# An S5 scan gated by a GeGLU block, rebuilt around token-major gates, DMA transposes and a planned engine order

## The chip, the cores and the metric

The kernel runs on one core of a Trainium2 chip. The metric is the device time of one execution in microseconds (us). Engine names: PE is TensorE, DVE is VectorE, ACT is ScalarE, POOL is GpSimd, SP is SyncE; SP computes nothing here and issues DMAs.

## The reference

x has 2048 tokens of 512 channels, bf16; the hidden width of the feed-forward block is 1376.

```python
xn = _layernorm(x)                                  # per token, no affine
Lam_bar = exp(dt * Lam)                             # 512 complex states
Bu = xn @ B_bar.T                                   # B_bar = ((Lam_bar - 1) / Lam)[:, None] * B
h[t] = Lam_bar * h[t-1] + Bu[t]                     # along 2048 tokens
s = 2 * (h @ C.T).real + xn * Dskip
g = silu((gelu(xn @ w_gate) * (xn @ w_up)) @ w_down)
out = x + s * g
```

## The kernel before

The tokens are cut into four slabs of 512 (`s`), each slab into four tiles of 128 tokens (`m`), and everything is done slab by slab. The complex recurrence is done as a real one: the rotation by the angle of `Lam_bar` is taken out with cosine and sine tables (`cos_b`, `sin_b`, L519 to L524), so that DVE's scan instruction (L382) runs on real and imaginary parts apart with the decay `rho`; a second rotation turns the result back into `hst`.

Per slab, in the order of the code: `u_pair` (L336) multiplies the normalised, transposed input `xnT` with `BT`, 32 matmuls, and ACT copies the result into `U` (L341); `chain` queues DVE's work on it (two products and two sums, L352 and L356, four scans, L382, and the same rotation again) for the two halves `h` of the states; `ffn` does the gates channel-major: for each of 11 blocks of 128 hidden channels four matmuls for gate (L418) and four for up (L423) with the 512 tokens as the moving operand, a Gelu and a copy on ACT (L428, L430), and a product on DVE (L431) which writes `at`, already with channels on the partitions as `down` needs them; `y_mm` makes `y` of the slab before with 8 matmuls from `hst` (L457) and 4 narrow ones which add the skip term by a diagonal matrix `diagI` (L462); `down` (L438) does 11 matmuls per token tile, then Tanh on ACT (L443) and a fused product on DVE (L445), which together are twice the silu; `epi` multiplies, adds x and stores (L475, L476, L479).

The order of PE, ACT and SP is the order of the code. DVE's order comes from a small hand-written clock: `dve()` issues a step at the PE time it was given, and `later()` keeps the scan's steps waiting until they fit in between. PSUM is three pools: four banks `mm`, two `f`, two `y`.

At the start, B's two halves come over ACT's queue (L91) and are transposed on PE (`b_transposes`, L142) while x, the small vectors, then the weights come over SP's queue; slab 0's first PE work of substance is `u_pair(0, 0)`, after its four tiles have been normalised (L164) and transposed on PE (L173). C is transposed by DMA on SP (L511), and so is the normalised input of slabs 1 to 3 (L506). A DMA from SP or ACT takes one of eight completion counters in turn, in the order in which both engines' DMAs stand in the program, and the ninth waits for the first to land: in listings of the order such a wait is written `waits DMAHW0_49`.

## Time and profile before

| | |
|---|---|
| median of 3 runs | 205.35 us (205.35 to 206.63) |
| span of the profiled execution, first to last instruction | 203.5 us |
| outside the span (median less span) | 1.85 us |
| PE, DVE, ACT busy | 184.6, 166.4, 114.5 us |

The profile is of one execution and its times are from the span's start; 1.85 us of the median lie outside of it. A busy PE is not PE at its peak: the profile's matmul durations overlap, so that PE's work is better read from the distance between starts. The chain of waits follows the execution back from its last instruction and says at each step what was waited for.

### The profile page before, as it was taken

How to read it: one execution, taken by the hardware profiler on the slowest of the kernel's cores; microseconds unless marked ns; L12 is line 12 of the kernel's file. 1: busy time of each engine (PE TensorE's matmuls, PEld its weight loads, DVE VectorE, ACT ScalarE, POOL GpSimd, SP SyncE). 2: the span in 40 equal slices, each digit the busy share in tenths (PEclk: the TensorE clock that was granted, in tenths of full speed). 3: DMA queues.
4: the chain of work that ended last, by engine and by line, in shares of the span. 5: the costliest groups of instructions: out<-in, count | busy, mean ns of one | idle time of the engine just before them, and what ended most of it. 6: DMA issues, size and time to landing. Idle time of an engine off the chain costs nothing.

```text
span 203.5 us, 2555 instructions
## 1 busy us (share of the span) xinstructions
PE 184.6 (91%) x903; PEld 86.6 (43%) x903; DVE 166.4 (82%) x283; ACT 114.5 (56%) x207; POOL 14.2 (7%) x31
## 2 busy tenths in 40 slices
PE   5617999996999999999599999999799999999992
PEld 1603344442444444454244444454344444454441
DVE  1427799999999898999999988999419999994443
ACT  2695486892777897751147997751256644441210
POOL 2001603100000015000000014000000000000000
PEclk9975799999999999999999999999999999999999
DMA  6999963220000000222000000231000000000001
GB/s 192 300 368 357 182 140 122 48 57 0 0 3 0 0 0 25 45 63 52 26 0 5 0 0 27 52 76 30 26 0 0 0 3 26 26 26 26 29 26 53
DMA packets 20988, 12.26 MB, mean 60 GB/s; under 512 B 11408, under 2 KB 20976, under 8 KB 20976
## 3 DMA queue, kind: packets, MB, share of 16 engines
q1 hardware_dynamic: 19920, 11.05, 19.7%
q10 hardware_dynamic: 1056, 1.05, 1.6%
q8 instruction: 7, 0.11, 0.2%
q14 instruction: 5, 0.04, 0.1%
HBM read 7.38 MB, written 2.10 MB: 47 GB/s over the span
## 4 chain that ended last, share of the span: by engine, by line
PE 43%; DVE 36%; ACT 14%; DMA 2%; issue 2%; POOL 1%; ACTq 0%
PE f_ps L438 13%; PE u_ps L336 10%; DVE Ft L382 7%; PE y_ps L457 7%; PE up_ps L423 6%; PE g_ps L418 6%; ACT junk L489 5%; DVE at L431 4%; DVE pp L352 3%; DVE qq L352 3%; DVE yg L475 3%; ACT ub L430 3%; DMA Bn<-in_A_B_re_dram 2%; DVE hst L356 2%; DVE Wt L356 2%
## 5 line engine op out<-in xcount | busy, mean ns | idle before, releaser
L418 PE MATMUL g_ps<-xnT,wg 128*128 128x512 bf16 (+1 forms) x176 | 45.2, 379 | 0.2 <-ACT gt L428 0.2
L423 PE MATMUL up_ps<-xnT,wu 128*128 128x512 bf16 (+1 forms) x176 | 45.2, 379 | 0.0
L438 PE MATMUL f_ps<-wd,at 128*128 128x512 bf16 (+1 forms) x176 | 39.4, 379 | 5.5 <-DVE g L445 3.2
L428 ACT ACTIVATE gt<-g_ps 128x512 bf16<-128x512 f32 (+1 forms) x44 | 26.2, 595 | 16.2 <-PE g_ps L418 14.0
L336 PE MATMUL u_ps<-xnT,BT 128*128 128x512 bf16 x128 | 30.8, 403 | 0.5 <-DVE xnT L211 0.5
L443 ACT ACTIVATE th<-f_ps 128x512 f32<-128x512 f32 x16 | 9.6, 597 | 38.5 <-PE f_ps L438 38.5
L382 DVE TENSOR_TENSOR_SCAN Ft<-rho,it,Wt 128x512 bf16<-128x512 f32 x24 | 30.4, 1275 | 0.0
L457 PE MATMUL y_ps<-C,hst 128*128 128x512 bf16 x128 | 30.2, 379 | 0.0
L430 ACT ACTIVATE ub<-up_ps 128x512 bf16<-128x512 f32 (+1 forms) x44 | 26.3, 597 | 7.0 <-PE up_ps L423 7.0
L438 PEld LDWEIGHTS <-at 128*128 128x128 bf16 (+1 forms) x176 | 17.0, 98 | 26.4 <-issue 3.7
L423 PEld LDWEIGHTS <-wu 128*128 128x128 bf16 (+1 forms) x176 | 17.6, 100 | 20.4
L418 PEld LDWEIGHTS <-wg 128*128 128x128 bf16 (+1 forms) x176 | 17.2, 100 | 18.7 <-issue 0.5
L341 ACT ACTIVATE U<-u_ps 128x512 bf16<-128x512 f32 x32 | 18.9, 597 | 9.2 <-PE u_ps L336 9.1
L431 DVE TENSOR_TENSOR at<-gt,ub 128x512 bf16<-128x512 bf16 (+1 forms) x44 | 18.0, 412 | 3.4 <-ACT ub L430 3.4
L336 PEld LDWEIGHTS <-BT 128*128 128x128 bf16 x128 | 13.2, 103 | 17.5 <-issue 3.8
L445 DVE SCALAR_TENSOR_TENSOR g<-th,f_ps 128x512 f32<-128x512 f32 x16 | 10.8, 679 | 11.0 <-ACT th L443 11.0
L457 PEld LDWEIGHTS <-hst 128*128 128x128 bf16 x128 | 12.3, 98 | 14.4 <-DVE hst L356 0.5
L475 DVE TENSOR_TENSOR yg<-y_ps,g 128x512 bf16<-128x512 f32 x16 | 10.9, 679 | 2.3 <-PE y_ps L462 2.2
L352 DVE TENSOR_TENSOR pp<-U,cos_b 128x2048 bf16<-128x2048 bf16 x8 | 9.8, 1220 | 2.9 <-ACT U L341 2.8
L356 DVE TENSOR_TENSOR hst<-pp,qq 128x1024 bf16<-128x1024 bf16 x16 | 10.6, 686 | 0.2
L356 DVE TENSOR_TENSOR Wt<-pp,qq 128x1024 bf16<-128x1024 bf16 x16 | 10.6, 685 | 0.1
L504 ACT ACTIVATE xn<-x_tok,nb,rs 128x512 bf16<-128x512 bf16 x12 | 9.7, 809 | 1.6 <-POOL nb L537 1.6
(104 smaller groups left out, 151.6 us busy)
## 6 DMA issues: line engine op xcount, KB each, us to landing
out_dram<-ot SPq DMA_DIRECT2D x16, 128.0 KB, 1.7
x_tok<-in_A_x_dram SPq DMA_DIRECT2D x3, 512.0 KB, 4.9
wd<-in_B_w_down_dram SPq DMA_DIRECT2D x1, 1280.0 KB
Bn<-in_A_B_re_dram ACTq DMA_DIRECT2D x1, 512.0 KB, 4.9
x_tok<-in_A_x_dram SPq DMA_DIRECT2D x2, 256.0 KB, 4.5
Bn<-in_A_B_im_dram ACTq DMA_DIRECT2D x1, 512.0 KB, 6.6
wg<-in_B_w_gate_dram SPq DMA_DIRECT2D x1, 512.0 KB, 5.7
wu<-in_B_w_up_dram SPq DMA_DIRECT2D x1, 512.0 KB
```

The costliest lines, as they stand in the source:

```text
L336: nc.tensor.matmul(u_ps[:, :], lhsT=BT[:, ri, kt, pt * P : (pt + 1) * P], rhs=xnT[:, kt, cols], start=(kt == 0), stop=(kt == KT - 1),)
L341: ACT(out=U[:, ri, q, :], in_=u_ps[:, :], func=AF.Copy)
L352: TT(out=box[key][:], in0=src()[:], in1=tab[:, hs, :].unsqueeze(1).to_broadcast(W), op=ALU.mult)
L356: return lambda: TT(out=dst()[i], in0=box["pp"][:, i, :, :], in1=box["qq"][:, 1 - i, :, :], op=op)
L382: nc.vector.tensor_tensor_scan(out=box["F"][:, ri, q, :], data0=rho[:, pt : pt + 1].to_broadcast([P, TS]), data1=box["W"][:, ri, q, :], in ...
L418: nc.tensor.matmul(g_ps[:fs, :], lhsT=wg[:, kt, fsl], rhs=xnT[:, kt, cols], start=(kt == 0), stop=(kt == KT - 1))
L423: nc.tensor.matmul(u_ps[:fs, :], lhsT=wu[:, kt, fsl], rhs=xnT[:, kt, cols], start=(kt == 0), stop=(kt == KT - 1))
L428: ACT(out=gt[:fs], in_=g_ps[:fs, :], func=AF.Gelu_apprx_tanh)
L430: ACT(out=ub[:fs], in_=u_ps[:fs, :], func=AF.Copy)
L431: dve(now() + 0.9, 0.34, lambda: TT(out=at[:fs, j, :], in0=gt[:fs], in1=ub[:fs], op=ALU.mult))
L438: nc.tensor.matmul(f_ps[:, :], lhsT=at[:fs, k, m0 : m0 + P], rhs=wd[:fs, k, :], start=(k == 0), stop=(k == NFT - 1))
L457: nc.tensor.matmul(y_ps[:, :], lhsT=hst[:, j // NPT, j % NPT, m0 : m0 + P], rhs=C2[:, j // NPT, j % NPT, :], start=(j == 0), stop=False,)
```

## The change

Nearly every line is new. What changes in the work:

- **Gates token-major.** A tile of 128 tokens is now the stationary operand and the weights move: per tile 4 x 2 matmuls over 512 columns, twice, and 4 x 2 over the last 352 columns (1376 = 512 + 512 + 352). The product `at` then has tokens on the partitions, and `at_t` turns it into `atT` with a DMA transpose on SP's queue (11 blocks of 128 x 128 per tile; slab 0 in pieces of 8 and 3).
- **Wide steps.** PSUM is three slots of two banks and two banks for `y`. ACT empties two banks with one instruction of 1024 elements; `down` does two tiles per slot; a rotation is one DVE product of 4096 elements and one sum of 2048 (in slab 0 two sums of 1024), with a table of four parts `tab`.
- **Silu** is one ACT instruction (in place of Tanh and the DVE product), with a table set other than Gelu's.
- **Skip term.** DVE makes `sk = xn * Dskip` per tile, ACT copies it into y's PSUM bank, and the 8 matmuls accumulate onto it; `diagI` and its matmuls are gone. The first two tiles add it on DVE.
- **Start.** B is transposed by DMA on SP's queue. ACT's queue brings the first two thirds of w_gate and w_up; POOL's queue brings the vectors, `Drow`, slab 1 of x, the last third and w_down. Slab 0's gates come before its `u`: tile 0 is only centred, transposed, and scaled by ACT as it leaves PSUM. `rs` and `rho` come from powers on POOL.
- **Order.** Each step is recorded with its engine, an assumed cost and what it reads and writes. `Plan.run` list-schedules them forwards and backwards in 12 rounds and emits the best schedule by start time. PE's order is that of the code; ACT's, DVE's, POOL's and SP's are the plan's.

The core of the diff (the recorder's calls are kept where they order the work):

```diff
+    def run(self):
...
+        for _ in range(ROUNDS):
+            start, length = self._pass(deps, [p + r for p, r in zip(prio, rank)], True)
...
+        for i in sorted(range(n), key=lambda i: (start[i], i)):
+            self.steps[i][2]()
...
-        th = work.tile([P, D], FP32, name="th", tag="th")
-        ACT(out=th[:], in_=f_ps[:, :], func=AF.Tanh, scale=0.5)
...
-        for kt in range(KT):
-            nc.tensor.matmul(
-                y_ps[:, kt * P : (kt + 1) * P], lhsT=xnT[:, kt, mg : mg + P], rhs=diagI[:, kt, :],
-                start=False, stop=(kt == KT - 1),
-            )
...
+    load_w(ACT, nc.scalar, 0, 4.5, not_before=0.72, rank=200.0)
...
+    slots = [psum.tile([P, 2, D], FP32, name=f"slot{i}") for i in range(3)]
+    ybank = [psum.tile([P, D], FP32, name=f"ybank{i}") for i in range(2)]
...
+    dummies(9)
+    stats(0, 0)
+    xc = xn[0]
+    dve(512, lambda: V.tensor_scalar(out=xc[:], in0=x_tok[:, 0, :], scalar1=mv[:, 0, 0, 0:1], scalar2=None, op0=ALU.subtract),
+        [("x", 0, 0), ("mv", 0, 0)], [("xc",)], rate=2.3)
+    transposed(xc, 0, xcT[:], [("xc",)], [("xcT",)], 0, DVE)
...
+        for kind, (nm, wt, dst) in enumerate((("wg", wg, gt[q]), ("wu", wu, ub[q]))):
+            i, ps = slot()
+            for c in range(2):
+                pe(KT, 512, mm(ps, c, wt, c), [("xnT", s % 2, m), (nm, c)], [("slot", i, c)])
+            fn = AF.Gelu_apprx_tanh if kind == 0 else AF.Copy
+            acts(1024, lambda ps=ps, dst=dst, fn=fn: act(out=dst[:, 0:1024].rearrange("p (c w) -> p c w", c=2), in_=ps[:, :, :], func=fn),
...
+    def at_t(s, m, c0, c1):
+        j = (s * M + m) % NAT
+        k0, k1 = CK[c0][0], CK[c1][1]
+        dma(SP, 0.3 * (k1 - k0), 1.6, lambda: nc.sync.dma_start_transpose(
+            out=atT[:, k0:k1, m * P : (m + 1) * P], in_=at[j][:, k0 * P : k1 * P]),
...
+        acts(1024, lambda: act(out=g2[gi][:, :, :], in_=ps[:, :, :], func=AF.Silu),
...
+        if seed:
+            acts(512, lambda: act(out=bank[:], in_=sk[s % 2][:, m, :], func=AF.Copy), [("sk", s % 2, m)], [("y", i)])
...
+                         start=(j == 0 and not seed), stop=(j == 2 * NPT - 1), skip_group_check=True)
...
+        def rot(src, table, reads):
+            dve(4096, lambda: V.tensor_tensor(out=Qf, in0=src.unsqueeze(1).to_broadcast(WQ), in1=table, op=ALU.mult),
+                reads, ["Q"], rate=2.0)
...
+            dma(SP, 1.3, 2.2, lambda ri=ri, k=k, src=src: nc.sync.dma_start(out=BT[:, ri, k, :], in_=src[:, k * P : (k + 1) * P], transpose=True),
...
+    load_w(ACT, nc.scalar, 1, 9.0, rank=199.0)
...
+    for m in range(M):
+        gate_pair(0, m, 0, (lambda m=m: head_t(m + 1)) if m + 1 < M else None)
...
+    load_w(POOL, G, 2, 5.0, not_before=6.5)
+    dma(POOL, 1.0, 5.0, lambda: G.dma_start(out=x_tok[:, M : 2 * M, :], in_=x_r[:, M : 2 * M, :]), writes=[("x", 1, m) for m in range(M)], not_before=6.5)
...
+    for m in range(2):
+        gate_pair(0, m, 1)
+    for h in range(2):
+        half(0, h)
...
+    for s in range(1, NS):
...
+        for m in range(M):
+            gate_tile(s, m)
+            at_t(s, m, 0, 2)
+            if not last and m > 0:
+                y_tile(s - 1, m - 1)
+                skip(s + 1, m - 1)
...
+        for h in range(2):
+            down_pair(s, h)
+    for m in range(M):
+        y_tile(NS - 1, m)
+    pl.run()
```

How the change moves instructions is shown at three places. First, the DMAs that SP issues at the start (`x_tok` is x, `hst1` holds C's transposes at this time). Before:

```order
L93 DMA x_tok<-in_A_x_dram 128x2x512 x2
L95 DMA pv<-in_A_log_dt_dram 4x128
L95 DMA pv<-in_A_Lambda_im_dram 4x128
L95 DMA pv<-in_A_Lambda_re_dram 4x128
L95 DMA pv<-in_A_Dskip_dram 4x128
L98 DMA wg<-in_B_w_gate_dram 128x4x384 [waits DMAHW0_49]
L99 DMA wu<-in_B_w_up_dram 128x4x384 [waits DMAHW1_49]
L101 DMA x_tok<-in_A_x_dram 128x4x512 [waits DMAHW2_49]
```

Now, on SP:

```order
L671 DMA_TRANSPOSE hst1_74<-in_A_C_re_dram 128x512
L246 DMA x_tok_63<-in_A_x_dram 128x512 x4
L671 DMA_TRANSPOSE hst1_74<-in_A_C_im_dram 128x512
L567 DMA_TRANSPOSE BT_69<-in_A_B_re_dram 128x512 [waits DMAHW0_49]
L567 DMA_TRANSPOSE BT_69<-in_A_B_re_dram 128x512 [waits DMAHW2_49]
L567 DMA_TRANSPOSE BT_69<-in_A_B_re_dram 128x512 [waits DMAHW3_49]
L567 DMA_TRANSPOSE BT_69<-in_A_B_re_dram 128x512 [waits DMAHW4_49]
L567 DMA_TRANSPOSE BT_69<-in_A_B_im_dram 128x512 [waits DMAHW5_49]
L362 DMA_TRANSPOSE xnT_64<-xn0_91 128x4x128 [waits DMAHW7_49,DVE_49]
L567 DMA_TRANSPOSE BT_69<-in_A_B_im_dram 128x512 [waits DMAHW0_49]
```

and on ACT's queue at the same time, where the two loads of `wg` are the second third and then the first:

```order
L251 DMA wg_66<-in_B_w_gate_dram 128x4x512 x2
L251 DMA wu_67<-in_B_w_up_dram 128x4x512 [waits DMAHW1_49]
L251 DMA wu_67<-in_B_w_up_dram 128x4x512 [waits DMAHW6_49]
L274 ACT_TABLE_LOAD
```

A transpose of C now stands ahead of x, the weights have moved to ACT's queue, and the first load of `wu` waits for counter 1, which that transpose of C holds.

Second, ACT around the sine and cosine of slab 0. Before:

```order
L208 ACTIVATE rho<-a_197 128x4 [waits DVE_49]
L225 ACT_TABLE_LOAD
L225 ACTIVATE sb<-ang 128x196 [waits DVE_49]
L226 ACTIVATE cb<-kr,halfpi 128x196 [waits DVE_49]
L341 ACTIVATE U<-u_ps 128x512 [waits PE_49] x8
```

Now (`slot0` to `slot2` are the PSUM slots, `U0` the first result of `u`):

```order
L581 ACT_TABLE_LOAD
L581 ACTIVATE sbt_136<-ang_134 128x196 [waits DVE_49]
L582 ACTIVATE cbt_137<-kr_135,halfpi_113 128x196 [waits DVE_49]
L397 ACTIVATE ub1_83<-slot0_106 128x512 [waits PE_49]
L397 ACTIVATE ub0_82<-slot1_107,rs_123 128x512 [waits PE_49,Activation_49]
L585 ACTIVATE cp_141<-cbt_137 128x128 [waits Activation_49]
L585 ACTIVATE sp_140<-sbt_136 128x128
L397 ACTIVATE ub0_82<-slot2_108 128x512 [waits PE_49]
L398 ACT_TABLE_LOAD
L398 ACTIVATE gt1_81<-slot0_106 128x512
L398 ACTIVATE gt0_80<-slot1_107,rs_123 128x512
L398 ACTIVATE gt0_80<-slot2_108 128x512
```

Three Gelus have moved behind the sines and behind a second table load, and `slot0`, which `u` writes next, is emptied by the first of them.

Third, DVE at the cosine's argument `kr`. Before:

```order
L223 TENSOR_TENSOR ang_230<-ang_230,kr_231 128x196 [waits DVE_49]
L224 SCALAR_TENSOR_TENSOR kr_231<-ang_230 128x196 [waits DVE_49]
L227 CAST sh_234<-sb_232 128x196 [waits Activation_49]
L228 CAST ch_235<-cb_233 128x196 [waits Activation_49]
L519 TENSOR_TENSOR t1__248<-ca_246,ch_235 128x2048 [waits Pool_49]
```

Now:

```order
L399 TENSOR_TENSOR at2_78<-gt1_81,ub1_83 128x512 [waits Activation_49]
L294 BN_STATS st_120<-x_tok_63 128x6 [waits DMASW4_49]
L580 SCALAR_TENSOR_TENSOR kr_135<-ang_134 128x196 [waits DVE_49]
L294 BN_STATS st_120<-x_tok_63 128x6 x3
L296 BN_AGGR mv_121<-st_120 128x2 [waits DVE_49] x4
```

`kr` now stands behind the first statistics of slab 1, which wait for a DMA from POOL's queue (`DMASW4`).

## Rows read from the trace of the kernel before

**Rows 1.** The page, engines: busy us, share of the span, instructions.
```profile
PE 184.6 (91%) x903; PEld 86.6 (43%) x903; DVE 166.4 (82%) x283; ACT 114.5 (56%) x207; POOL 14.2 (7%) x31
```
**Rows 2.** The chain of waits in order of time: start us, us, what.
```profile
0.72 4.90 DMA Bn<-in_A_B_re_dram
...
13.92 1.28 ACT L160
15.21 0.21 ACT rs L160
...
141.90 1.20 DVE hst L356 x2
...
148.66 6.91 PE u_ps L336 x32
...
165.93 0.22 PE y_ps L462 x4
...
199.46 0.24 PE y_ps L462 x4
```
**Rows 3.** Windows: us, busy PE PEld DVE ACT POOL, granted clock, DMA share, GB/s.
```profile
12.00:16.00 4.00, 0.08 (x2) 0.08 (x2) 0.55 (x2) 3.92 (x7) 0.00 (x0) 0.57 1.08 370
20.00:22.00 2.00, 2.00 (x6) 0.70 (x5) 0.25 (x1) 0.76 (x2) 2.00 (x2) 0.50 1.29 259
...
50.00:60.00 10.00, 8.76 (x41) 4.02 (x42) 9.93 (x16) 6.65 (x12) 0.00 (x0) 1.00 0.01 2
...
90.00:100.00 10.00, 7.89 (x41) 3.61 (x40) 9.93 (x16) 2.40 (x5) 0.00 (x0) 1.00 0.14 39
```
**Rows 4.** Timeline of the start: start us, us, engine, line, what, idle before.
```profile
5.64 0.39 SPq L98 DMA_DIRECT2D wg<-in_B_w_gate_dram  x1
15.86 5.88 SPq L511 DMA_TRANSPOSE CT<-in_A_C_re_dram  x4
17.67 2.72 PE L336 MATMUL u_ps<-xnT,BT 128*128 128x512 bf16 x6 [0.52 <-DVE xnT L211]
21.66 1.90 POOL L241 COPY sa<-sh 128x2048 bf16<-128x2048 bf16 x1
21.75 2.91 DVE L519 TENSOR_TENSOR t__248<-ca,ch 128x2048 bf16<-128x2048 bf16 x1 [1.99 <-POOL ca L240]
```
**Rows 5.** Groups by line and shape: busy us, mean ns of one, idle before.
```profile
L145 ACT ACTIVATE BT<-tb_ps 128x1024 bf16<-128x1024 bf16 x4 | 3.9, 1015 | 3.4 <-PE tb_ps L142 3.4
L430 ACT ACTIVATE ub<-up_ps 128x512 bf16<-128x512 f32 x40 | 23.9, 598 | 6.4 <-PE up_ps L423 6.4
L445 DVE SCALAR_TENSOR_TENSOR g<-th,f_ps 128x512 f32<-128x512 f32 x16 | 10.8, 679 | 11.0 <-ACT th L443 11.0
L352 DVE TENSOR_TENSOR pp<-U,cos_b 128x2048 bf16<-128x2048 bf16 x8 | 9.8, 1220 | 2.9 <-ACT U L341 2.8
L356 DVE TENSOR_TENSOR hst<-pp,qq 128x1024 bf16<-128x1024 bf16 x16 | 10.6, 686 | 0.2
L281 DVE SCALAR_TENSOR_TENSOR C<-CT,cre,tA 128x512 bf16<-128x512 bf16 x4 | 3.0, 743 | 0.0
L382 DVE TENSOR_TENSOR_SCAN Ft<-rho,Wt 128x512 bf16<-128x512 f32 x8 | 9.4, 1207 | 0.0
```
**Rows 6.** DMAs: the page's issues to landing, and the transposes of xnT.
```profile
x_tok<-in_A_x_dram SPq DMA_DIRECT2D x3, 512.0 KB, 4.9
Bn<-in_A_B_im_dram ACTq DMA_DIRECT2D x1, 512.0 KB, 6.6
CT<-in_A_C_re_dram SPq DMA_TRANSPOSE x4, 5.4
...
L506 SPq DMA_TRANSPOSE xnT<-xn x12: 1188/1196/2017, 37.3 to 136.6; - x12
...
DMA to landing us min/median/max: 2.4/2.5/3.1
```

More of the change, by code (lines that the diff above doesn't have):

```diff
@@ L2 @@
 from contextlib import ExitStack
+import heapq
 import math
@@ L88, with pool, dma @@
+    def pool(cost, emit, reads=(), writes=(), **kw):
+        return pl.add(POOL, cost, emit, reads, writes, lag=0.08, **kw)
+    def dma(eng, issue, land, emit, reads=(), writes=(), **kw):
+        return pl.add(eng, issue, emit, reads, writes, lag=land, **kw)
+    x_r = A_x[0].rearrange("(m p) d -> p m d", p=P)
+    out_td = out[0]
     wg_r = B_w_gate.rearrange("(k p) f -> p k f", p=P)
     wu_r = B_w_up.rearrange("(k p) f -> p k f", p=P)
-    for ri, src in enumerate((A_B_re, A_B_im)):
-        nc.scalar.dma_start(out=Bn[:, ri, :, :], in_=src.rearrange("(k p) d -> p k d", p=P))
@@ new lines, in transposed, with f @@
+    def transposed(src, n, dst, reads, writes, bank, evict):
+        tp = ybank[bank][:].bitcast(BF16)[:, 0:D].rearrange("p (k t) -> p k t", t=P)
+        def f():
+            for k in range(KT):
+                T.transpose(tp[:, k, :], src[:, k * P : (k + 1) * P], ident[:])
+        pe(KT, P, f, reads + ["ident"], [("y", bank)])
+        if evict == ACT:
+            acts(512, lambda: act(out=dst, in_=tp, func=AF.Copy), [("y", bank)], writes, rank=40.0)
+        else:
+            dve(512, lambda: V.tensor_copy(out=dst, in_=tp), [("y", bank)], writes, rate=2.0, rank=40.0)
@@ new lines, in head_t @@
+    def head_t(m):
+        transposed(xn[m], m, xnT[:, :, m * P : (m + 1) * P], [("xn", m)], [("xnT", 0, m)], m % 2, DVE)
+    for m in range(1, M):
+        stats(0, m)
+        rstd(0, m, m + 1)
+        norm_dve(0, m)
+    tables()
+    for m in range(M):
+        gate_pair(0, m, 0, (lambda m=m: head_t(m + 1)) if m + 1 < M else None)
+    norm_dve(0, 0)
+    dma_t(0, 0)
+    dma(POOL, 1.0, 3.0, lambda: G.dma_start(out=Drow[:], in_=A_Dskip.partition_broadcast(P)), writes=["Drow"], rank=-20.0)
@@ L509 @@
+    coefficients()
     for ri, src in enumerate((A_C_re, A_C_im)):
         for pt in range(NPT):
[L511 to L519 removed]
```

935 lines of the change are left out of this document (510 added, 425 removed).

## The prediction

> **What bounds the kernel now.** Read the engines' busy times first: PE 91% and DVE 82% of the span [rows 1]. Two such shares do not say which one sets the time, so go to the chain of waits in the last slab: from the first `u` matmul of slab 3 at 148.66 us to the last matmul's end at 199.46 + 0.24 = 199.70 every piece is PE [rows 2], and 32 matmuls of 512 columns take 6.91, that is 0.216 each; four of 128 columns take 0.22, or 0.055 each. Count the work at these prices: 784 matmuls of 512 columns (176 gate, 176 up, 176 down, 128 `u`, 128 `y`) are 169.3, the 64 skip matmuls 3.5, together 172.8. PE's first `u` starts at 17.67 [rows 4]; 17.67 + 172.8 = 190.5, and PE ends at 199.70, so 9.2 us are lost on the way. The windows show where: in slab 0 and at the ends of slabs 0 and 1 PE is busy 8.76 and 7.89 of 10 us while DVE is busy 9.93 of 10, so 3.4 us of waits for DVE stand in these two windows alone [rows 3]; and the first `u` matmuls run at 2.72 / 6 = 0.45 each [rows 4] with a granted clock of 0.50, the 1.2 GHz level, after a window in which PE was busy 0.08 of 4 us and the clock fell [rows 3]. The span is then 17.67 before PE's main work, 182.0 of it, and 203.5 - 199.7 = 3.8 of tail (last product, sum, store). The median, 205.35, lies 1.85 above the span, and I add the same to the new one.
>
> **PE's work after.** 128 matmuls of 352 columns replace 96-row and 512-column ones: 16 tiles x 16 gate matmuls of 512 columns, 128 `u`, 128 `y`, 176 down make 688 x 0.216 = 148.6; the 352-column ones are 128 x 0.148 (by columns) = 19.0; 16 transposes of the start 0.9. Together 168.5, which is 4.3 less than before, nearly all of it the skip matmuls (3.5).
>
> **Where PE's work starts.** No row shows the new start, so I walk it, bounding each step.
> 1. ACT's queue: the order has the second third of `wg` first, then the first third, as B's two halves stood before. The second of those landed 6.6 after its issue [rows 6]; issued about 1.2, this is 7.8, and with C's transposes beside it about 8.3. `x` is there before that. Gate 0 starts about 8.3.
> 2. `wu`'s first third cannot be issued until counter 1 is free, and that is held by the first transpose of C. That such a wait binds is in the trace: `wg` was issued at 5.64 [rows 4], when the DMA issued at 0.72 had landed after 4.90 [rows 2]. A transpose lands 2.5 (quiet) to 5.4 (under load) after issue [rows 6], so `wu` is issued at 3.2 to 6.1 and lands 4.9 to 6.6 later: 8.1 to 12.7. I take 11, near the loaded ends, since the queues are full. PE waits for it after gate 0.
> 3. From there to the end of six gate-and-up pairs: 44 matmuls x 0.216 and 8 transposes, 9.9. For the clock: nothing if it stays at the 2.4 GHz level, up to 2.5 if, as after 17.67 before, some 5 us run at 1.2 GHz. I take 1.3, halfway, because this PE is idle for shorter stretches than the 4 us which preceded the fall [rows 3]. PE is through at 22.2.
> 4. `u` wants `slot0`, which a Gelu behind the sines empties. Behind the sixth pair ACT still does a copy (0.60 [rows 5]), a table load (1.28; the activation behind it starts right then [rows 2]) and the Gelu (0.60), with two hand-overs about 2.8: `u` starts at **25.0**. The Trainium skill, ScalarE: Activation LUTs, "What ACT_TABLE_LOAD costs", adds a drain to the load and gives 2.66 in all; by that 26.4 and a sum 1.4 higher. The trace has none: 13.92 + 1.28 = 15.20, next activation 15.21 [rows 2].
> 5. B's transposes: from about 5.6 (counter 0 frees when the first `wg` lands), 8 x 1.47 (5.88 / 4 [rows 4]) and one of 1.2 [rows 6]: issued by 18.6, landed by 22.3 to 24. Just hidden behind 25.0.
>
> PE has 11.0 of its 168.5 behind it at 25.0 and 157.5 ahead: 182.5 without a wait.
>
> **Waits after that.** *DVE in slab 0.* Its tables can start at 26.7 (two products behind the Gelus). Up to the last fold of C it has 6 products of 2048 at 1.22, four of 4096 at 2.29 (1.22 plus twice the 0.534 between 1024 and 2048 elements), eight sums at 0.69, eight scans at 1.21, eight folds at 0.74 [rows 5] and small ones for 3.5: 41 in all; consecutive steps overlap by 0.09 (two sums take 1.20 [rows 2], not 1.37), which makes 37; with up to 3 of waiting for ACT's scaled C, 64 to 67. PE wants `y` of slab 0 at 25.0 + 40.8 = 65.8. I take 1.3 of waiting; bounds 0 and 3. Behind PE's `y` the gates of two tiles are queued, and ACT and DVE live from those.
> *DVE later.* It drops 16 products for the silu (10.9 [rows 5]), and per half rotation four instructions become two: about 4.5 in all; it gains 16 skip products of about 0.42: 166.4 [rows 1] becomes about 158. Some 17 of it lie before 26.7 and 7 behind its last sum, so that sum is done at 26.7 + 134 = 161 if DVE never waits; with 8 of waiting for slab 3's gates, 169. PE wants it four `y` tiles (6.9) before its end at 184.5, at 177: no wait, a cushion of 8.
> *ACT.* Eviction of two banks is 1.02 (1015 ns for 1024 elements [rows 5]) against 2 x 0.60, while PE needs 1.73 for two banks: hidden. The added copies into `y`'s banks (14 x 0.60) and six more table loads fall where PE is in `down`, 4.75 per slot; that cover gone, a load would cost 1.28. Only the last seeds are tight: a product must leave the bank, then ACT copies, while PE is in the other bank for 1.73; 0.68 + 0.60 + hand-overs is about that. 0.7 in all.
> *SP.* A four-block transpose takes SP 1.2 and lands after 2.5 [rows 6]. By blocks, eleven take 3.3 and land after 4.6. Per slab SP then has 4 x 3.3 + 4 x 1.2 + stores, about 19 of 42 us. The wait for them falls between a slab's last gate and its `down`; PE has 6.9 of `u` or `y` there, and 4.75 more before tiles 2 and 3. Bounds: 1.2 (no growth) to 4.0 (C's rate); either is hidden.
>
> **Sum.** 25.0 + 157.5 + 1.3 + 0.7 + 3.8 = 188.3 span; + 1.85 = **190 us**, 15 less than 205.35: 4.3 from less PE work, 3.7 from the start (11.0 done by 25.0 is as if PE had begun at 14.0), 7.2 from waits and slow clock (9.2 before, 2.0 after).
>
> **Rivals.**
> - *A, forecast*: PE never waits long. 186 to 194, with the cold stretch, `wu` and the slab 0 wait at their bounds. 0.55.
> - *B, late loads*: `kr` waits behind slab 1's statistics, these for x from POOL's queue, and all of ACT's row behind the cosine for `kr`. I expect x at about 17 (issued about 12, 4.9 to land [rows 6]); from about 19.5 on every us is lost. For it: DMA shares above 1 at the old start [rows 3], and a DVE product beside a POOL copy took 2.91 where its like takes 1.22 [rows 4, 5], so the two engines do get in each other's way. Five to eight us late: 194 to 200. The Trainium skill, SBUF — State Buffer, "SBUF: two separate sides", says that DMAs from POOL's queue stall while DVE holds the port they share, as their descriptors are written there; that is this rival. No run here shows a DMA from that queue. 0.17.
> - *C, slow turns*: eleven blocks cost 6.6, not 3.3. Then the fourth tile of the last slab lands some 4 us after `down` wants it: 194 to 195; in the other slabs `u` hides it. 0.06.
> - *D, better start*: the clock stays up and `wu` lands at 9: 183 to 186. 0.12.
> - *E, the other side*: DVE does not run the 4096-element product at two elements per cycle, which its broadcast input and table in four parts may prevent. Against it: the same kind of product, with a broadcast table, did (1.22 for 2048). Each would cost 2.1 more, 16 of them 34. DVE is then the bound: its last sum comes at 26.7 + 134 + 34 = 195, four `y` tiles (6.9), the tail (3.8) and 1.85 follow: 207. From 0.5 more per product on (the cushion of 8) PE waits. With only slab 0's products affected it is 197. 0.10, with what I have not thought of.
>
> Range 184 to 198: it leaves out E, half of D and the slowest of B. This kernel's measurement can tell about 1% from no change: faster by that 0.90, within it 0.03, slower 0.07, the last two from E.
>
> **What would show it.** First gate matmul at about 8 and first `u` at about 25; granted clock 0.50 for at most 5 us after that first gate; DVE's 4096-element product at 2.3; ACT's 1024-element evictions at 1.0; SP's eleven-block transposes at 3.3; PE without idle time from slab 1 on. I am wrong if `u` starts after 29 (B), if PE waits for `atT` (C), or if DVE's rotation takes 4 (E).

## The result and the profile after

The changed kernel takes **194.2 us** (median of four runs, 193.35 to 195.64) against 205.99 for the kernel before on the same chip: 0.945 of it, interval 0.939 to 0.950. The forecast was 190 with a range of 184 to 198. The profiled execution has a span of 193.7 and a time of 195.64, 1.94 outside the span; all that follows is made against this span, which the forecast put at 188.3. It is the longest of the four (the others 193.35 to 194.73), so a span set beside its 193.7 can show up to 2 us that the medians do not. The ratios leave out executions more than 1.5% longer than the fastest of their kernel: two of four in gelu_behind_up (197.6 and 198.5), two of six in head_last, one of four each in x_first and all_head.

The page's busy times answer to [rows 1]: PE has 6.0 us less, DVE 8.9 less, ACT 5.9 more, POOL twice as much.

```profile
PE 178.6 (92%) x826; PEld 83.3 (43%) x842; DVE 157.5 (81%) x250; ACT 120.4 (62%) x176; POOL 30.5 (16%) x48
```

The chain of waits in order of time (start us, us, what) answers to [rows 2]. From 30.54 on it holds nothing but PE until the last product; everything that is not PE lies ahead of that.

```profile
2.02 5.55 DMA x_tok<-in_A_x_dram
...
28.59 1.28 ACT L398
...
183.56 6.00 PE ybank L474 x27
...
189.59 0.70 DVE yg L480
```

PE's own timeline of the start (start us, us, engine, line, what, idle before) answers to [rows 4]. L316 is the transpose of a tile, L390 a gate or up matmul of slab 0, L514 `u`.

```profile
8.96 0.61 PE L316 MATMUL ybank<-ident,xn 128*128 128x128 bf16 x4 [3.70 <-DVE xn L330]
...
10.09 1.89 PE L390 MATMUL slot<-wg,xcT 128*128 128x512 bf16 x4 [0.40 <-DVE xcT L321]
12.57 0.61 PE L316 MATMUL ybank<-ident,xn 128*128 128x128 bf16 x4 [0.60 <-DVE xn L356]
14.09 1.87 PE L390 MATMUL slot<-wu,xcT 128*128 128x512 bf16 x4 [0.91 <-ACT gt L398]
...
18.35 1.85 PE L390 MATMUL slot<-wu,xnT 128*128 128x512 bf16 x4 [0.26 <-ACT gt L398]
20.01 1.06 PE L390 MATMUL slot<-wg,xnT 128*128 128x512 bf16 x4
...
21.75 0.81 PE L390 MATMUL slot<-wu,xnT 128*128 128x512 bf16 x3 [0.46 <-ACT gt L398]
...
26.93 1.03 PE L390 MATMUL slot<-wu,xnT 128*128 128x512 bf16 x4
30.54 8.62 PE L514 MATMUL slot<-xnT,BT 128*128 128x512 bf16 x31 [2.58 <-ACT gt L398]
```

Four matmuls of 512 columns take 1.9 us up to 20.0 and 1.03 behind it: the first half of the start runs at the lower pace. The windows around `u` (us, busy PE PEld DVE ACT POOL, granted clock, DMA share, GB/s) answer to [rows 3]:

```profile
30.00:32.00 2.00, 1.46 (x4) 0.55 (x4) 1.27 (x4) 2.00 (x4) 0.00 (x0) 0.57 1.32 240
32.00:34.00 2.00, 2.00 (x6) 0.69 (x5) 2.00 (x3) 0.25 (x1) 0.00 (x0) 0.57 1.42 149
```

After the idle 2.58 us the clock falls near its 1.2 GHz level for some 4 us, and `u`'s 31 matmuls take 8.62. The page's groups that answer to [rows 5], and its DMA issues that answer to [rows 6]:

```profile
L514 PE MATMUL slot<-xnT,BT 128*128 128x512 bf16 x124 | 29.6, 394 | 2.8 <-ACT gt L398 2.6
...
L528 DVE TENSOR_TENSOR Q<-U,tab 128x4096 bf16<-128x4096 bf16 x8 | 18.3, 2287 | 0.2
...
L470 ACT ACTIVATE ybank<-sk 128x512 f32<-128x512 bf16 x14 | 8.4, 602 | 12.8 <-DVE yg L480 7.3
L421 ACT ACTIVATE gt<-slot 128x1024 bf16<-128x1024 f32 x12 | 12.3, 1022 | 4.5 <-PE slot L413 4.3
...
x_tok<-in_A_x_dram SPq DMA_DIRECT2D x4, 128.0 KB, 5.0
x_tok<-in_A_x_dram POOLq DMA_DIRECT2D x1, 512.0 KB, 5.1
```

The turns of `at` on SP's queue, by their line (ns min/median/max of the issue, first and last start; then us to landing):

```profile
L438 SPq DMA_TRANSPOSE atT<-at x20: 1178/1335/1759, 32.1 to 167.5; - x20
...
DMA to landing us min/median/max: 2.3/3.5/5.1
```

**Where the time went.** Before, 17.67 of start, 172.8 of work, 9.2 lost and 3.8 of tail made 203.5. Now PE has 11.0 of work behind it at 30.54 (it stands as if it had begun at 19.5), then the other 157.5, 1.6 for the slow clock at `u`, and a tail of 193.7 - 189.56 = 4.1. Of the 9.8 us gained, 4.3 are PE's work and 7.6 waits and slow clock; the start gives back 1.9 and the tail 0.3. The gain behind `u` is what was forecast; the start, which was to bring 3.7, costs 1.9.

Of the 9.2 lost in the kernel before, 5.5 were waits of PE's `down` for DVE, more than half of them for the product of the silu, which is now on ACT (line, for whom: us, times, longest):

```profile
PE f_ps L438 <- DVE g L445: 3.2, 2, 2.1
...
PE f_ps L438 <- DVE at L431: 2.3, 2, 1.8
```

From its first `u` on PE now waits for nothing that the profile names. No run undoes the silu alone, so that its move took the 3.2 away is likely, but not shown.

### The profile page after: what moved, and what is told of

It is laid out like the page before. It is cut to its first block, busy times and chain, and to the rows that moved or that the text cites. A ratio compares the mean times of both kernels' runs of the same rounds, so it can differ in the third digit from the quotient of the medians.

```text
span 193.7 us, 2403 instructions
## 1 busy us (share of the span) xinstructions
PE 178.6 (92%) x826; PEld 83.3 (43%) x842; DVE 157.5 (81%) x250; ACT 120.4 (62%) x176; POOL 30.5 (16%) x48
## 4 chain that ended last, share of the span: by engine, by line
PE 89%; DMA 3%; ACT 3%; DVE 1%; issue 1%; SPq 1%; ACTq 0%
PE slot L413 29%; PE slot L455 20%; PE slot L514 15%; PE ybank L474 14%; PE slot L390 12%; DMA x_tok<-in_A_x_dram 3%; ACT L398 1%; ACT gt L398 1%; SPq L671 1%; DVE st L294 0%; DVE yg L480 0%; PE ybank L316 0%; DVE xcT L321 0%; DVE ot L488 0%; DVE xn L330 0%
## 5 line engine op out<-in xcount | busy, mean ns | idle before, releaser
L413 PEld LDWEIGHTS <-xnT 128*128 128x128 bf16 x288 | 28.1, 98 | 28.6
L455 PE MATMUL slot<-wd,atT 128*128 128x512 bf16 (+1 forms) x173 | 38.5, 379 | 0.2
L514 PE MATMUL slot<-xnT,BT 128*128 128x512 bf16 x124 | 29.6, 394 | 2.8 <-ACT gt L398 2.6
L413 PE MATMUL slot<-wu,xnT 128*128 128x512 bf16 (+1 forms) x144 | 31.8, 357 | 0.0
L413 PE MATMUL slot<-wg,xnT 128*128 128x512 bf16 (+1 forms) x140 | 31.6, 356 | 0.2
L547 DVE TENSOR_TENSOR_SCAN Fs<-rho,ini,W 128x512 bf16<-128x512 f32 x24 | 29.1, 1265 | 0.0
L474 PE MATMUL ybank<-C,hst 128*128 128x512 bf16 x124 | 28.4, 379 | 0.2
L455 PEld LDWEIGHTS <-atT 128*128 128x128 bf16 (+1 forms) x176 | 17.2, 98 | 20.9
L514 PEld LDWEIGHTS <-BT 128*128 128x128 bf16 x128 | 12.9, 101 | 18.9 <-issue 4.4
L528 DVE TENSOR_TENSOR Q<-U,tab 128x4096 bf16<-128x4096 bf16 x8 | 18.3, 2287 | 0.2
L528 DVE TENSOR_TENSOR Q<-Fs,tab 128x4096 bf16<-128x4096 bf16 x8 | 18.3, 2286 | 0.1
L470 ACT ACTIVATE ybank<-sk 128x512 f32<-128x512 bf16 x14 | 8.4, 602 | 12.8 <-DVE yg L480 7.3
L390 PEld LDWEIGHTS <-xnT 128*128 128x128 bf16 x72 | 7.5, 104 | 8.7 <-issue 2.9
```

Source lines behind the costliest of these rows:

```text
L390: T.matmul(ps[:, bank, 0:w], lhsT=lhs(k), rhs=wt[:, k, a:b], start=(k == 0), stop=(k == KT - 1))
L413: T.matmul(ps[:, bank, 0 : b - a], lhsT=xnT[:, k, t0 : t0 + P], rhs=wt[:, k, a:b], start=(k == 0), stop=(k == KT - 1))
L455: T.matmul(ps[:, b, :], lhsT=atT[:fs, k, m * P : (m + 1) * P], rhs=wd[:fs, k, :], start=(k == 0), stop=(k == NFT - 1))
L470: acts(512, lambda: act(out=bank[:], in_=sk[s % 2][:, m, :], func=AF.Copy), [("sk", s % 2, m)], [("y", i)])
L474: T.matmul(bank[:, :], lhsT=hst[s % 2][:, j // NPT, j % NPT, m * P : (m + 1) * P], rhs=C2[:, j // NPT, j % NPT, :], start=(j == 0 and not ...
L514: T.matmul(ps[:, ri, :], lhsT=BT[:, ri, k, pt * P : (pt + 1) * P], rhs=xnT[:, k, (s % 2) * TS : (s % 2 + 1) * TS], start=(k == 0), stop=(k ...
```

## The experiments

My theory after the result: PE is the bound from `u` on, and the 5.5 us by which `u` is late (30.54, forecast 25.0) are x's late first tile, the lower pace, and the waits for ACT, each of which can be taken away by itself. The rival: the loads or DVE hold slab 0 anyway, so what the start gains is lost again behind `u`.

Most kernels here keep the changed kernel's plan and move single recorded steps in its order before they are emitted; a list of moves names the steps by their place in the recording:

```diff
-        for i in sorted(range(n), key=lambda i: (start[i], i)):
+        seq = sorted(range(n), key=lambda i: (start[i], i))
+        for names, where, anchor in self.moves:
...
+        for i in seq:
```

Lines of these kernels stand 8 to 10 further down. Spans are of the profiled execution, beside 193.7 for the changed kernel. Unless another view is named, a block shows PE's timeline.

**x_first.** x's four loads go ahead of the first transposes of C in SP's queue.

```diff
+    pl.moves = [((196, 200), "ahead", 197)]
```

> The four issues of x for slab 0 stand ahead of C's first two transposes on SP's queue; the two transposes stand just ahead of C's third. Nothing else is moved. Theory (x's late landing sets the first gate): x's first tile is issued at about 0.7 instead of 2.02 and lands at about 6.3 instead of 7.58; the first gate matmul follows 2.5 later, at 8.8 instead of 10.09, the first u at about 29.3 instead of 30.54, and the span falls from 193.7 to about 192.4. Rival (the DMA engines are full, so what x gains the first thirds of wg and wu lose): first gate within 0.3 of 10.09 and the span within 0.5 of 193.7.

Span 191.5, ratio 0.939 (0.932 to 0.946); `u` at 28.46, 2.1 earlier.

```profile
4.75 0.40 PE L324 MATMUL ybank<-ident,xn 128*128 128x128 bf16 x4
8.15 0.17 PE L343 MATMUL ybank<-ident,pv 12*128 12x12 bf16 x1 [3.00 <-DMA pv<-in_A_Lambda_re_dram]
8.24 1.89 PE L398 MATMUL slot<-wg,xcT 128*128 128x512 bf16 x4
```

x is turned 4.2 us earlier, but PE then waits for the parameters, whose small transpose stands ahead of the gates; only 1.85 of the 4.2 reach the first gate. The whole gain at `u` is in the span: B's last transpose lands at 23.4, well ahead of 28.46. By the ratios, 0.939 against 0.945, the gain is about 1 us, and the intervals overlap.

**dummies.** 23 warm-up matmuls (on a tile of zeros, their result is not read) in place of 9.

```diff
-            for _ in range(k):
+            for _ in range(k + 14):
```

> Fourteen more of the dummy matmuls stand behind the nine at the start, so that PE has work from 1.24 until about x's first transposes; nothing else is moved. Theory (the gates' low pace, 1.89 for four matmuls, follows from PE's idle stretch from 5.26 to 8.96): four gate matmuls take about 1.0 from the first one on, the six pairs are through about 4 earlier, at about 24, and the first u starts at about 27.1, held there by B's last transpose, which landed at 27.0; span about 190.3. Rival (the pace rises at a certain time after the start, about 20, whatever PE does before): four gate matmuls still take 1.89, first u at 30.5 or, if the dummies run over, up to 1 later; span 193.7 to 194.7.

Span 192.2, ratio 0.946 (0.941 to 0.952); `u` at 29.19. Its timeline, and the windows of the same stretch:

```profile
9.90 1.04 PE L390 MATMUL slot<-wg,xcT 128*128 128x512 bf16 x4 [0.42 <-DVE xcT L321]
12.39 0.61 PE L316 MATMUL ybank<-ident,xn 128*128 128x128 bf16 x4 [1.45 <-DVE xn L356]
13.06 1.86 PE L390 MATMUL slot<-wu,xcT 128*128 128x512 bf16 x4
```

```profile
10.00:12.00 2.00, 0.94 (x4) 0.21 (x3) 1.56 (x7) 1.57 (x3) 1.92 (x4) 0.89 1.14 339
12.00:14.00 2.00, 1.55 (x7) 0.84 (x8) 1.62 (x6) 1.00 (x2) 1.83 (x5) 0.50 1.31 250
```

The first gates run at full pace; then PE is idle 1.45 us, the granted clock falls to 0.50, and full pace is back only at 18.69. Of the 3.4 that I expected at `u` 1.35 came in this execution, and nothing by the ratios, 0.946 against 0.945. The warm-up gains the first gates and no more.

**gelu_behind_up.** The three Gelus that PE's up matmuls waited for are emitted behind those matmuls; no engine's own order changes.

```diff
+    pl.moves = [((79,), "behind", 77),
+                ((86,), "behind", 84),
+                ((93,), "behind", 91)]
```

A Gelu reads one bank of a slot while the up matmul writes the other, but the wait is kept by slot, so the one emitted first holds the other back. PE's row of the first up matmul before and after the move:

```order
L390 MATMUL slot0_106<-wu,xcT 128x512 [waits Activation_49]
L398 MATMUL slot0_106<-wu,xcT 128x512 [waits DMAHW1_49]
```

> In the program the Gelus of the first three pairs stand behind these pairs' up matmuls instead of ahead of them; PE's own order is the same. Theory (gate and up share one slot, and an up matmul that stands behind the slot's Gelu waits for it, though it writes the other bank): the waits of 0.91, 0.26 and 0.46 ahead of the first three groups of up matmuls go, the six pairs are through at about 26.4 instead of 27.96, the first u starts at about 28.9, and the span is about 192.1. Rival (something else, such as wu, would end these waits hardly earlier, or the Gelu behind the sines takes it back): first u within 0.4 of 30.54, span 193.3 to 194.

Span 188.8, ratio 0.931 (0.923 to 0.939); `u` at 27.19, 1.7 earlier than expected.

```profile
13.18 1.91 PE L398 MATMUL slot<-wu,xcT 128*128 128x512 bf16 x4
14.88 1.30 PE L398 MATMUL slot<-wg,xnT 128*128 128x512 bf16 x4
...
16.25 1.03 PE L398 MATMUL slot<-wu,xnT 128*128 128x512 bf16 x4
...
27.19 7.07 PE L522 MATMUL slot<-xnT,BT 128*128 128x512 bf16 x31 [2.58 <-ACT gt L406]
```

The three waits were 1.63 us, yet 3.35 are gained at `u`: the full pace is there from about 16 on, not from 20.0. And behind the same idle 2.58 the clock doesn't fall this time, which gives 1.55 more. 3.35 + 1.55 is the span's 4.9 in this execution; the ratios, of two executions here, give some 2.8.

That the pauses had held the pace down is not shown. In skip_on_pe (below) PE has no pause from 14.10 on, and four matmuls take 1.9 us up to 19.6:

```profile
14.10 1.87 PE L389 MATMUL slot<-wu,xcT 128*128 128x512 bf16 x4 [0.91 <-ACT gt L397]
...
17.89 1.91 PE L389 MATMUL slot<-wu,xnT 128*128 128x512 bf16 x4
```

**gelus_first.** The last three Gelus of the start stand ahead of the sines, so that `u` needn't wait for a table.

```diff
+    pl.moves = [((98,), "behind", 97),
+                ((115,), "behind", 114),
+                ((120,), "behind", 119),
+                ((60, 64, 61, 62, 63, 65), "behind", 120),
+                ((194, 195), "behind", 128)]
```

> On ACT the Gelus of the fourth, fifth and sixth pair stand right behind their up copies, and the sine and cosine with their table load behind the sixth; DVE's coefficients stand behind the first product of the rotation. Theory (the 2.58 in front of the first u are the Gelu behind the sines, and DVE in slab 0 is the next in line): first u at about 28.0 without a wait, but DVE's tables still start at about 32, since the sines now come at about 30.5; DVE's last fold of C stays at about 72.8, and PE, which would want the first y of slab 0 at about 69 to 70.5, waits there for 2.5 to 4; span 193.2 to 194.2. Rival (DVE has the 6 to 8 us to spare that it has in the last slab): no wait ahead of y, span 189.4 to 191.1.

Span 195.3, ratio 0.958 (0.953 to 0.963).

```profile
27.97 5.34 PE L522 MATMUL slot<-xnT,BT 128*128 128x512 bf16 x24
37.25 0.58 PE L522 MATMUL slot<-xnT,BT 128*128 128x512 bf16 x1 [3.93 <-ACT U L525]
```

`u` starts 2.57 earlier without a wait, and stops after 24 matmuls for 3.93: ACT's evictions of `U` now stand behind the sines and slab 1's normalization, which waited for POOL. I had put that wait on DVE, at slab 0's `y`; there PE doesn't wait. The number was near, the place wrong. The sines have to go the other way.

**sines_first.** gelu_behind_up, with the sines and what makes their angles moved to the idle time of ACT and DVE before the first Gelu. ACT's order, beginning: Sin table, sines, Gelu table, then Gelus and copies only; two table loads fewer.

```diff
...
+                ((98,), "behind", 97),
+                ((115,), "behind", 114),
+                ((120,), "behind", 119),
+                ((56,), "behind", 32),
+                ((57, 58, 59, 60, 61, 63, 65), "behind", 47),
+                ((64, 62), "behind", 105),
...
```

> Holds the edit of the run with the Gelus behind the up matmuls (first u at 27.19 there, after 2.58 of waiting for the Gelu behind the sines; span 188.8), and moves more: DVE's four angle steps right behind the first normalized tile, sine, cosine and their two copies on ACT ahead of the first Gelu, where the table of the sines is in ACT already, so that two table loads fall away; two of DVE's table products behind the copy of tile 2, the rest behind slab 1's statistics, DVE's coefficients behind the first rotation product, and ACT's first u eviction ahead of slab 1's normalization. Theory (the wait ahead of u is the Gelu behind the sines, and the sines can be had early for nothing): PE is through with the pairs at 24.4 and then waits only for B's last transpose, which landed at 25.7 in that run; first u at 25.8, no wait ahead of the first y of slab 0, span about 187.4. Rival (as with the Gelus first: something else is late instead, the copies of x behind DVE's products or the eviction of u): first u after 27 or waits behind it of over 1.5 in all, span 188.8 or more.

Span **186.9**, time **188.8 us** (188.5 to 189.4), ratio 0.920 (0.918 to 0.923): 5.4 less than the changed kernel by the medians, and no other run is measurably faster.

```profile
20.15 1.04 PE L398 MATMUL slot<-wg,xnT 128*128 128x512 bf16 x4 [1.31 <-DVE xnT L329]
...
25.34 7.07 PE L522 MATMUL slot<-xnT,BT 128*128 128x512 bf16 x32
```

`u` starts at 25.34 without a wait, and its stretch to the end is 161.6 = 157.5 of work + 4.1 of tail: PE doesn't wait once behind it. The span falls by 5.2 at `u` + 1.6 of slow clock = 6.8, to the digit. Neither DVE nor B takes anything back (B's last transpose is issued at 18.0 and lands at 23.6).

**all_head, head_again, head_last.** Three tries to stack x_first and warm-up matmuls (8, 4, 4 of them behind x's transpose) on sines_first, with the parameters' transpose behind the first gates; in the second, `wu`'s first third is also issued ahead of `wg`'s second, and in the third ACT's, DVE's and PE's orders are moved further. In these two the first two Gelus stand ahead of the sines again, at two more table loads. Of their moves, a line of the first, of the second and of the third each:

```diff
+                ((101,), "behind", 41),
...
+                ((4, 5), "ahead", 42),
...
+                ((105,), "ahead", 30),
```

> The run with the sines first, and in addition: x ahead of C's transposes, B's transposes ahead of that of tile 0, the parameters' transpose behind the first gate instead of ahead of it (it held that gate until 8.15 in the run with x first), eight dummy matmuls behind x's first transposes, the first two reciprocal roots ahead of the step size's power on GpSimd. Theory (each of these is a wait of the start, and they add up): first gate at about 7.2, when the first third of wg has landed (7.05), the pairs through at 19 to 20, first u at about 22, when B has landed (23.4 with x first, one issue of 1.3 earlier here); from there as in the run with the Gelus behind the up matmuls (161.6 to the end of the span): 183.6. Rival (DVE is next in slab 0: its first rotation cannot start before about 30, its last fold of C comes at 64 to 66, while PE wants the first y at 63): a wait of 1 to 3 there, span 184.6 to 186.6.

> The run with the sines first, with the start put in another order, by what held PE in the two runs before it: x ahead of C's transposes, the first thirds of wg and wu ahead of their second thirds (in both runs the first up matmuls came when wu's first third had landed, at 12.1 to 12.6), tile 1's transposes and then the parameters' behind the first up, each copy and normalization of x ahead of the statistics that wait for a later tile of x, DVE's first table products behind the copy of tile 3 (that copy stood behind them and PE waited 1.31), four dummies behind x's first transposes, slab 1's normalization behind two evictions of u, and two of C's transposes and the first turn behind slab 1's x on SP. The first two Gelus come ahead of the sines, at two more table loads. Theory (these waits are all that is left of the start, and PE is the bound behind it): first gate at about 6.1, first u at 19 to 21, B's last transpose landing at 19 to 20 (14.6 + 5.5 in the run before), 161.6 from there: span 181 to 183. Rival (something later is then late instead: DVE ahead of slab 0's first y, or slab 1's x, for which u waited 1.1 in the run before): waits of 2 or more behind the first u, span 184 to 187.

> The start once more, by what held PE in the run before (first u at 24.17, span 187.4, although the first gate stood at 6.12): ACT had been kept from its first Gelu until 15.2, since the issue of wu's second third ahead of it waited until 11.98 for a counter; that issue now stands behind the second Gelu. DVE's normalization of tile 3, which waits for GpSimd, stands behind the copy of tile 2 and the angle steps instead of ahead of them (PE waited 1.44 for that copy); slab 1's x is issued before the step size's power on GpSimd, its statistics stand ahead of DVE's table products, and all of U's first half is evicted around them as planned before. Theory (these waits, 4.6 on PE between the first gate and the first u in that run, are what is left): first u at 21 to 22, then 161.6 to the end; span 182.6 to 184. Rival (slots: the Gelus between the sines' two table loads set when the fourth to sixth pair may be written, and the start is at its end): first u at 23.5 or later, span 185.5 to 187.

| | span | ratio | first gate | `u` | waits over 1 us between the first gate and `u` |
|---|---|---|---|---|---|
| sines_first | 186.9 | 0.920 (0.918 to 0.923) | 10.39 | 25.34 | copy of tile 3: 1.31 |
| all_head | 188.4 | 0.924 (0.920 to 0.928) | 7.69 | 25.57 | parameters 1.22, tile 1's `xn` 1.23, copy of tile 3 1.31 |
| head_again | 187.4 | 0.919 (0.911 to 0.927) | 6.12 | 24.17 | `wu` 1.51, copies 1.46 and 1.44 |
| head_last | 189.9 | 0.929 (0.923 to 0.936) | 7.00 | 28.27 | `wu` 1.59, copy 1.05, `wu`'s second third 4.24 |

All three of my figures for `u` (22, 19 to 21, 21 to 22) were too early, and none of the three beats sines_first measurably. The first gate can stand at 6 to 8, but what follows it comes no earlier: the weights and DVE's preparation of the tiles. all_head also starts slab 1's `u` behind a wait of 1.06 for its x. In head_last the order of the issues is the cause. PE's timeline, then ACT's queue:

```profile
24.15 1.87 PE L400 MATMUL slot<-wu,xcT 128*128 128x512 bf16 x4 [4.24 <-DMA wu<-in_B_w_up_dram]
```

```profile
17.82 0.37 ACTq L259 DMA_DIRECT2D wu<-in_B_w_up_dram  x1
```

That load was issued at 17.82: its issue waited for a completion counter on which B's transposes now stood, and ACT's work stood behind it (the profile marks ACT's next step `3.47 <-DMA BT<-in_A_B_im_dram`). The earliest `u` of these runs is 24.17; what holds the start there, and what a better division of the queues would give, is open.

**product_twice.** DVE's eight products of U with the table are made twice: 18.3 us more of DVE's work.

```diff
-            dve(4096, lambda: V.tensor_tensor(out=Qf, in0=src.unsqueeze(1).to_broadcast(WQ), in1=table, op=ALU.mult),
+            dve(4096, lambda: [V.tensor_tensor(out=Qf, in0=src.unsqueeze(1).to_broadcast(WQ), in1=table, op=ALU.mult)
+                               for _ in range(2 if src is not Ff else 1)], reads, ["Q"], rate=2.0)
```

> The changed kernel with the first 4096-element product of each half rotation done twice: eight products of 2.29 more for DVE, 18.3 in all; nothing else is moved. Theory (DVE has no room in slab 0, where its last fold of C ended 0.24 before the first y matmul at 72.94, and 4 to 6 us per slab after that): PE waits for about 4.3 ahead of the first y of slab 0 and nowhere else; span 198.0. Rival (DVE's room was used up over the whole run: 157.5 of 193.7 busy, 6.3 to spare ahead of the last slab's y): PE waits in every slab, 12 in all, span 205 to 206. The other rival (DVE has 6 or more to spare everywhere): span 193.7.

Span 201.3, ratio 0.990 (0.988 to 0.993). From `u` to the end it takes 171.3 against 163.2: 8.1 of the 18.3 reach PE, between the two theories. The waits of PE (line, for whom: us, times, longest):

```profile
PE slot L413 <- ACT gt L421: 3.2, 3, 1.3
...
PE slot L413 <- ACT g L459: 2.3, 2, 1.8
...
PE ybank L474 <- ACT ybank L470: 1.4, 1, 1.4
```

The three rows are 6.9 of the 8.1. PE meets DVE's lateness through ACT, whose copies into `y`'s banks and evictions come late; ACT's own waits for DVE ahead of those copies grow from 7.3 (the group of L470 above) to 19.7:

```profile
ACT ybank L470 <- DVE yg L480: 19.7, 9, 5.1
```

At slab 0's `y` itself, where I had looked, PE doesn't wait. By this, DVE had about 10 us to spare over the four slabs.

**turned_twice.** In slabs 1 to 3 every turn of `at` is issued twice, 12 more transposes on SP's queue; the second of a pair is issued only when the first has landed.

```diff
-        dma(SP, 0.3 * (k1 - k0), 1.6, lambda: nc.sync.dma_start_transpose(
+        dma(SP, 0.3 * (k1 - k0), 1.6, lambda: [nc.sync.dma_start_transpose(
-            out=atT[:, k0:k1, m * P : (m + 1) * P], in_=at[j][:, k0 * P : k1 * P]),
+            out=atT[:, k0:k1, m * P : (m + 1) * P], in_=at[j][:, k0 * P : k1 * P]) for _ in range(2 if s else 1)],
```

> The changed kernel with each turn of the gates' product by DMA in slabs 1 to 3 issued twice, the second one after the first has landed, so that every tile of 11 blocks is there about 4.8 later (1.3 of issue and 3.5 to land). Theory (the turns are hidden behind u or y and behind down of the tiles ahead, 5 us and more in the last slab): PE does not wait for them, span within 0.5 of 193.7, first u to end as before. Rival (the turn is near its limit, as in the case of slow turns in the prediction): PE waits ahead of down in the last slab or in each, 3 to 12 in all, span 197 to 206.

Span 197.6, ratio 0.970 (0.965 to 0.975).

```profile
91.63 8.75 PE L514 MATMUL slot<-xnT,BT 128*128 128x512 bf16 x32 [3.02 <-DMA xnT<-xn]
```

`down` never waits for `atT`, even so. What is late is slab 2's x, whose transposes stand behind the turns on the same queue: 3.0 of wait and 1.5 of slow clock behind it. SP's queue has room for the turns once, not for such pairs.

**u_first.** The changed kernel with slab 0's `u` ahead of its gates, planned anew.

```diff
-    for m in range(M):
-        gate_pair(0, m, 0, (lambda m=m: head_t(m + 1)) if m + 1 < M else None)
+    for m in range(1, M):
+        head_t(m)
...
-    for m in range(2):
-        gate_pair(0, m, 1)
     for h in range(2):
         half(0, h)
-    for m in range(2, M):
-        gate_pair(0, m, 1)
+    for c in range(2):
+        for m in range(M):
+            gate_pair(0, m, c)
```

> One part of the change undone: in slab 0 the u matmuls stand ahead of all gates, the six pairs that stood ahead of them follow; the planner orders everything else anew. Theory (PE is the bound from u on, so what it has behind it by then is what the gates first are worth): u waits for B's last transpose, which landed at 25.7 to 27.0 in the other runs, with only transposes (0.9) behind PE; 26 + 167.6 of PE's work + 1.7 for a stretch at the low pace + 4.1 of tail make a span of about 199.4, 5.7 more than 193.7. Rival (with the gates away from the loads and from ACT, B lands earlier and DVE begins its rotation earlier, which gives it back): u at 20 to 22, span 193 to 195.5.

Span 195.1, time 199.0 (197.1 to 199.9), ratio 0.966 (0.956 to 0.975). The profiled execution is the fastest of the four; its span is the rival's, the median, some 197 as a span, lies between the theories.

```profile
17.48 2.72 PE L514 MATMUL slot<-xnT,BT 128*128 128x512 bf16 x6 [0.51 <-DVE xnT L321]
...
23.04 7.21 PE L514 MATMUL slot<-xnT,BT 128*128 128x512 bf16 x24 [2.00 <-DMA BT<-in_A_B_im_dram]
30.09 1.03 PE L390 MATMUL slot<-wg,xcT 128*128 128x512 bf16 x4
```

`u` starts about where it did before, at 17.48, stops for B, and behind 30.09 PE doesn't wait. Gates first is worth 4.8 by the medians (199.0 against 194.2, 2% by the ratios): the smaller part of the gain. The spans, 195.1 against 193.7, show less, being of the fastest execution here and the longest there. The waits for DVE in slab 0 [rows 3] don't come back with `u` first, so what took them away lies in the rest of the change (the wide steps, Silu on ACT); which part of it, these runs don't separate.

**skip_on_pe.** The skip term goes back to PE (four matmuls of 128 columns per tile with `diagI`); `sk`, DVE's products and ACT's copies are gone. The start was planned anew and differs (`u` at 28.20).

```diff
-            acts(512, lambda: act(out=bank[:], in_=sk[s % 2][:, m, :], func=AF.Copy), [("sk", s % 2, m)], [("y", i)])
...
+            for k in range(KT):
+                T.matmul(bank[:, k * P : (k + 1) * P], lhsT=xnT[:, k, t0 : t0 + P], rhs=diagI[:, k, :],
+                         start=False, stop=(k == KT - 1), skip_group_check=True)
```

> One part of the change undone: the skip term is again added by four 128-column matmuls per y tile against a diagonal matrix (64 in all), instead of ACT's copy of DVE's product into the bank; for that the normalized and turned x is kept for three slabs. The copies (14 of 0.60 on ACT) and the products (16 of 0.42 and two sums of 0.69 on DVE) fall away; the planner orders anew. Theory (PE's work counts one for one, and neither ACT nor DVE was waited for): 64 x 0.055 = 3.5 more from the first u to the end of the span, 166.7 instead of 163.2; span 197.2. Rival (the copies and products were on the path as well, by the 0.7 that the prediction took for them or more): 165.5 or less from the first u to the end.

Span 193.8, ratio 0.947 (0.938 to 0.955).

```profile
187.30 0.39 PE L474 MATMUL ybank<-diagI,xnT 128*128 128x128 bf16 x4
```

From `u` to the end it takes 165.6, against 161.6 without a slow clock (sines_first): 4.0, near the 3.5 by PE's prices, as it would be if PE's work counts one for one. (The 166.7 that I expected held the 1.6 of slow clock at `u`, which this execution doesn't have.) By the ratios, 0.947 against 0.945, nothing is left of it: `u` starts 2.3 earlier here, and its 1.6 of slow clock is missing.

## Why the prediction was right, and where not

- **PE's work and the stretch behind `u`: right.** Forecast 163.3 from `u` to the span's end (157.5, 1.3, 0.7, 3.8), measured 163.2, but of other parts: no wait for DVE or for the last seeds, and 1.6 of slow clock that I hadn't put there. The agreement to 0.1 is luck: 2.0 of waits that didn't come against 1.6 of slow clock and 0.3 more of tail. sines_first shows the 157.5 of work as it is, skip_on_pe the price of more.
- **DVE in slab 0:** 1.3 of waiting forecast, none measured, and by little: DVE's last fold of C ends at 72.70, PE's first `y` starts at 72.94. Both came later than forecast, as `u` did.
- **Where PE's work starts: the step that failed**, 25.0 against 30.54.
  - Gate 0 at 8.3: it came at 10.09 (+1.8). I took `wg` for the last to arrive and wrote that x is there before that. x's first load stands behind a transpose of C in SP's queue, is issued at 2.02 and lands 5.55 later, at 7.58, when `wg` is there (issued at 1.2, landed 5.8 later). Behind it statistics, centring, transpose and copy take 2.5 more, which step 1 put at nothing. x_first, with x earlier, has `u` 2.1 earlier.
  - `wu` at 11, PE waiting for it: it did land about then, but PE's up matmul was held at 14.09 by the Gelu of the same slot. The idle time of this stretch is 2.23 against my 1.84; the size is near, the cause another. A wait that the diff's text doesn't show was in the row of PE's order.
  - The clock: 1.3 taken, up to 2.5 allowed, 4.6 measured (15.64 us of busy PE for 11.0 of work). This is the mis-sized term, +3.3. I argued that shorter idle stretches than 4 us leave the clock up; PE was idle 3.70 ahead of x's transposes, and the gates behind run at the lower pace to 20.0. dummies, which fills most of that stretch, has the first gates at full pace. When the pace comes back differs (16 in gelu_behind_up, 20 in skip_on_pe), and by what is open.
  - The hand-over to `u`: 2.8 forecast, 2.58 measured, right. The table load again has no drain behind it: it starts at 28.59, takes 1.28, and the Gelu begins at 29.89. The Trainium skill, ScalarE: Activation LUTs, "What ACT_TABLE_LOAD costs", gives 2.66 with a drain; this trace disagrees as the one before did.
  - Together: 1.8 + 0.4 + 3.3, 0.2 for four transposes of tiles that step 3 left out, and 0.2 less at the hand-over, are the 5.5.
- **E, the wide product: out.** 2.287 us for 4096 elements, as costed at 2.29 [rows 5]. product_twice shows what about half of the rival's 34 us would have cost: 18.3 more of DVE's work, 8.1.
- **B, late loads: didn't happen**, although its sign, `u` after 29, did. x for slab 1 landed 5.1 after its issue, and its statistics began at 23.78 right behind DVE's other work. That sign told lateness, not its cause. The Trainium skill, SBUF — State Buffer, "SBUF: two separate sides", says that loads from POOL's queue stall while DVE holds the port they share; this trace shows no such stall, but DVE was busy only 0.62 of the 4 us from 14 to 18, so it is no test.
- **C, slow turns: out.** The twelve turns of eleven blocks take 1.38 each on SP's queue and land after 3.5 (3.3 and 4.6 forecast; the row above holds slab 0's pieces too); PE never waits for `atT`.
- **D, a better start:** not in this kernel, and no run reaches its 183 to 186. sines_first comes nearest with 188.8, and that by other means than an early `wu`.
- **DVE's cushion** at the end: 8 forecast. Its last sum ends at 176.2 and PE wants it at 182.48, 6.3.
- **The clock's sign** (0.50 for at most 5 us after the first gate) was wrong: it stood low for some 10 us by the pace of the matmuls, and again for 4 at `u`.

The total came out in the range because the stretch behind `u`, 84% of the span, was counted from rows, while the start was walked with one guess (the clock) and one order not read (x's load). At 194.2 it lies just past the upper end of A's 186 to 194, without B's cause.

## What to carry to other kernels

Once one engine is busy without a gap from some point on, the span is that point plus its work, and in sines_first every us gained ahead of that point arrives whole; so price the steady part from rows and spend the effort on the start. In a start, follow each operand to its issue and each matmul to its waits in the engine's order, since two halves of one buffer can wait for each other where their data do not: taking 1.63 of such waits away brought 3.35 at `u` in gelu_behind_up. Move work into the idle time of the engine that does it (the sines ahead of the first Gelu), and look each time at what is then queued behind it.
